# First loads of q and k by pairs of tiles, turned by 64x64 products, and second heads' v shifted by one chunk

## The chip, the cores and the metric

The kernel runs on one core of one Trainium2 chip. The metric is device time in microseconds (us) of one execution. Three executions of the kernel before took 480.24, 480.55 and 480.69 us, a median of 480.55. One more execution was taken with the hardware profiler.

A core has a matrix engine (PE, or TensorE), three engines for elementwise work (DVE or VectorE, ACT or ScalarE, POOL or GpSimd), and an engine that here only issues transfers (SP). Each has its own instruction stream. In this kernel every engine works through its stream in the order in which the program was written; an instruction that has to wait holds up all that stands behind it on its engine.

## The reference

Two stages, one behind the other, all in fp32:

```python
# q, k, v: 8 batches, 8 heads, 576 tokens, 64 numbers a head; chunks of 64 tokens
scores = matmul(q_c, k_c.transpose(0, 1, 2, 4, 3)) / 8       # inside each chunk
attn   = exp(scores - max(scores)); attn /= sum(attn) + 1e-9
x      = matmul(attn, v_c)              # rearranged to 4608 tokens x 512
h      = x @ w_in                       # 512 -> 1024
e      = exp(h - max(h))
solu   = h * e / (sum(e) + 1e-9)
ln     = (solu - mean(solu)) / sqrt(var(solu) + 1e-6) * g_ln
out    = ln @ w_out                     # 1024 -> 512
```

w_in and w_out come as 64-bit floats, so they are 4 MB each.

## The kernel before, in words

The 4608 tokens are 36 **tiles** of 128 tokens: two chunks of 64 tokens, all 8 heads. A tile passes through these steps, named by the word that stands for each in the list `START`, which orders the first tiles by hand; behind the word comes the tile.

- `n`: q and k of a tile are loaded in natural layout, one token a partition, all heads beside one another. In DRAM a head's tokens lie one behind the other, so that each packet of the load is one token of one head: 64 numbers, 256 bytes.
- `N`: four 128x128 transposes on PE (`po<-ident,nat`, two heads in each) for q or for k, and one copy out of PSUM to `qT` or `kT`, on ACT, or on DVE for the pairs in `NV_DVE`.
- `S`: scores, 16 products of 64x64 (`sx<-kT,qT`). `A`: maximum, subtraction (both DVE) and exponential (ACT). `B`: sum and reciprocal (DVE), then the product with it (POOL).
- `T`: the weights are transposed on PE (`po<-ident,e`) and copied to `attn_t`. `V`: 16 products with v (`sy<-attn_t,v_sb`), and the copy of the result: to `x_f` for tiles 0 and 1, else split in a high and a low part, `x_h` and `x_l`.
- `v`: the load of v. `T` leaves the weights of half of the heads, here the second heads of the pairs, with the tile's two chunks swapped over the partitions. For tiles 0 to 5 v is therefore loaded in three transfers: the first heads over 128 partitions, and the second heads in two of 64 partitions each, swapped (four in tile 4, where the batch ends in the middle).
- `M`: h of a tile, into both banks of `ph`, of which there is one. Tiles 0 and 1 use 8 fp32 products `ph<-w_a,x_f`; from tile 2 on three reduced-precision products stand for one, 24 in all (`wi_l,x_h`, `wi_h,x_h`, `wi_h,x_l`). M of tile 0 comes in four pieces, one for each quarter of the weights, so that it can start before all of them are there.
- `X`, `Y`: maximum of h (DVE `h_nmax`), exponential (ACT `z`), product with h (DVE `z`), and the scaling. The next tile's `M` needs `ph`, so it waits for the product on DVE.
- `z`, `Z`: the transposing of z; `F`: the products with w_out (`po<-wo_h,z_h` and so on).
- `P`, `P0`, `P1`: loads of the weights (`w_raw`, 1 MB each; 0 comes in two halves). `c`, `C`, `t`, `D` turn 64-bit floats to fp32 and split them: `c` is a clamp on `w_raw` (DVE or POOL, by `CL_DVE`) and a pass on ACT, `C` a shift and a `SCALAR_TENSOR_TENSOR` on DVE, `t` and `D` the high and low parts. `g` and `G` load and turn g_ln.
- `W`: two 128x128 products of the identity whose result nobody reads, into one held `ph` tile.

A word that stands several times in `START` goes on with its step where it had stopped: `N:0:1` the second time is the copy. Word order sets the order on every engine and of SP's transfers at once. Behind `START` a loop over tiles 5 to 35 does the rest; from there on q and k come in the packets of 128 bytes (`q_st`, `k_st`) and are turned on DVE, and the loop is not touched by the change.

All instructions pass through one helper, so that the profile puts them at line 50; they are told apart by the names of their tiles. `po` is two tiles of one PSUM bank, `ph` one tile of two banks, `sx` and `sy` one tile each.

Of the kernel before, what the change touches and what calls it, by code (L numbers as in the profile page):

```python
# [21 lines left out]
N:2:1 T:0 N:2:1 A:1 C:1 C:0 B:1 V:0 B:1 P:3 N:3:0 t:2 S:2 N:3:1 V:0 M:0 A:2 N:3:0 c:3 N:3:1 T:1  # L22
T:1 S:3 D:2:1 P:4 n:4 c:3 v:1 M:0 A:3 G C:3 A:2 n:5 M:0 G C:3 c:4 M:0 P:5 A:3 B:2 N:4:1 N:4:0
t:3 c:4 n:6 B:2 N:4:1 v:2 N:4:0 V:1 v:3 B:3 B:3 X:0 T:2 T:2 P:6 X:0 Y:0 C:4 N:5:0 C:4 S:4 N:5:0
D:2:0 A:4 V:1 c:5 P:7 T:3 T:3 D:3:0 N:5:1 M:1 t:1 D:1:0 N:5:1 V:2 t:4 A:4 c:5 t:0 D:4:0 N:6:1
D:4:1 D:0:0 N:6:0 C:5 B:4 Y:0 V:2 n:7 X:1 B:4 D:1:1 N:6:1 V:2 X:1 S:5 N:6:0 T:4 D:0:1 V:3 T:4
Y:1 v:4 z:0:0 n:8 D:3:1 z:0:1 A:5 z:0:1 C:5 z:0:0 c:6 z:0:0 M:2 A:5 N:7:0 R:0 B:5 v:7 V:3 B:5
t:5 v:5 Q:2 q:8 z:0:1 c:6 T:5 S:6 V:3 D:5:0 V:4 X:2 C:6 N:7:0 N:7:1 T:5 q:8 c:7 X:2 F N:7:1 C:6
V:4 Y:2 N:8:0 c:7 t:6 D:5:1 C:7 M:3 V:4 C:7 N:8:0 D:6:0 Y:2 N:8:1 t:7 q:8 D:7:0 Y:1 D:6:1 A:6
N:8:1 V:5 D:7:1 X:3 n:9 S:7 Z:2 R:2 z:1:0 F A:7 X:3 Y:3 A:7 z:1:0 F B:7 Y:3 A:6 V:5 o:0 M:4 B:7  # L30
z:1:1 v:6 B:6 Z:3 o:0 z:1:1 z:1:0 z:1:1 B:6 R:3 X:4 F V:5 N:9:0 N:9:0 X:4 F N:9:1 U:6 U:7 R:1 F
Y:4 o:1 N:9:1 Y:4 o:1 R:4 q:8
"""


# [23 lines left out]
def chunk_attention_then_solu_ffn(  # L59
# [178 lines left out]
    AT = const.tile([P, 2, 2, H, 32], F32, name="attn_t")  # L240
# [61 lines left out]
    def load_v(i):  # L302
        V[i] = work.tile([P, H, D], F32, name="v_sb", bufs=4)
        if i < TURNS:

            parts = [(0, p0, p1, b, s) for p0, p1, b, s in tile_parts(i)]
            for c in range(2):
                b, n = chunk_of(i, c)
                parts.append((1, (1 - c) * CH, (2 - c) * CH, b, n * CH))
            for j, p0, p1, b, s in parts:  # L310
                sync.dma_start(
                    V[i][p0:p1, j * HP:(j + 1) * HP, :],
                    v[b, j::2, s:s + p1 - p0, :].rearrange("h t d -> t h d"),
                )
# [593 lines left out]
```

## Time and profile before

| | |
|---|---|
| runs | 480.24, 480.55, 480.69 us |
| profiled execution | 481.02 us |
| its span, first to last instruction | 479.2 us |
| PE busy | 464.7 us, 97% of the span |
| DVE, ACT, POOL busy | 363.9 us (76%), 251.7 us (53%), 157.4 us (33%) |
| chain that ended last | PE 91%, DMA 4%, SP's queue 3% |
| transfers | 195076 packets, 72.57 MB, mean 151 GB/s |

The profiled execution takes 1.8 us more than its span, for what lies before the first and behind the last instruction. A row of the timeline gives the start, the time from there to the end of the group, the engine, and the operation as out<-in; what the engine stood idle before it and what ended that is in brackets. An fp32 product of PE appears as two records (the 16 products of S are x32, the 8 of M of tile 1 are x16), a transpose and a reduced-precision product as one. Beside PE's busy share, PEclk gives the clock that was granted to it, as a part of full speed. The first 60 us are the ones to look at: there PE stands still or waits for a part of the time, and from there on the chain of waits is PE with hardly a break.

### The profile page before, as it was taken

The numbers are of one execution on the slowest core, as the hardware profiler recorded it, in microseconds if no ns is written. First come the engines' busy times: TensorE is split into PE (matmuls) and PEld (weight loads), VectorE is DVE, ScalarE is ACT, GpSimd is POOL, SyncE is SP. The second block draws the span as 40 slices with busy tenths as digits, with TensorE's granted clock in tenths as the row PEclk, the third lists the DMA queues.
The fourth block names the chain that finished last, engine by engine and source line by source line (L and its number), as shares of the span: only waits on it lengthen the run. The fifth ranks groups of instructions, "written<-read, shape, count | busy, mean of one in ns | idle before, by whom it ended". The sixth has DMA issues, their size and how long they took to land.

```text
span 479.2 us, 11042 instructions
## 1 busy us (share of the span) xinstructions
PE 464.7 (97%) x4189; PEld 380.1 (79%) x4189; DVE 363.9 (76%) x508; ACT 251.7 (53%) x406; POOL 157.4 (33%) x304
## 2 busy tenths in 40 slices
PE   5699999999999999999999999999999999999997
PEld 5556788888888888888888888888888888888876
DVE  1879986697878787878787878797979797945430
ACT  2668784546454645454545555454545455554451
POOL 1255557350505050505050505032515141413300
PEclk9799999999999999999999999999999999999999
DMA  9998999787886878596348595958644434334211
GB/s 265 261 231 216 255 137 195 169 194 156 176 174 168 155 179 145 147 174 165 83 131 163 135 186 124 190 134 180 149 111 111 112 104 118 98 101 112 66 45 44
DMA packets 195076, 72.57 MB, mean 151 GB/s; under 512 B 179208, under 2 KB 179728, under 8 KB 194640
## 3 DMA queue, kind: packets, MB, share of 16 engines
q1 hardware_dynamic: 188608, 59.15, 55.8%
q0 software_dynamic: 6272, 12.60, 10.2%
q8 instruction: 33, 0.54, 0.5%
q14 instruction: 19, 0.16, 0.1%
q10 hardware_dynamic: 144, 0.13, 0.1%
HBM read 37.23 MB, written 9.44 MB: 97 GB/s over the span
## 4 chain that ended last, share of the span: by engine, by line
PE 91%; DMA 4%; SPq 3%; issue 1%; DVE 0%; ACT 0%; DVEq 0%; ACTq 0%
PE po L50 43%; PE ph L50 39%; PE sx L50 5%; PE sy L50 3%; SPq L50 3%; DMA nat<-in_q_dram 3%; DMA nat<-in_k_dram 1%; DMA v_sb<-in_v_dram 1%; ACT z L50 0%; DVE h_nmax L50 0%; ACT z_h L50 0%; DVE o_sb L50 0%; DVE z L50 0%; DVEq L50 0%; ACTq L50 0%
## 5 line engine op out<-in xcount | busy, mean ns | idle before, releaser
L50 PE MATMUL po<-wo_l,z_h 128*128 128x512 f32 x280 | 111.1, 397 | 0.1
L50 PE MATMUL po<-wo_h,z_l 128*128 128x512 f32 x280 | 109.6, 391 | 0.0
L50 PE MATMUL po<-wo_h,z_h 128*128 128x512 f32 x280 | 109.3, 390 | 0.0
L50 ACT ACTIVATE z<-ph,h_nmax 128x1024 f32<-128x1024 f32 x36 | 40.2, 1118 | 130.3 <-DVE h_nmax L50 130.0
L50 PE MATMUL ph<-wi_l,x_h 128*128 128x512 f32 x272 | 106.0, 390 | 0.0
L50 PE MATMUL ph<-wi_h,x_h 128*128 128x512 f32 x272 | 105.8, 389 | 0.0
L50 POOL TENSOR_TENSOR u<-ssq,eps 128x1 f32<-128x1 f32 x36 | 6.8, 190 | 215.8 <-ACT sq L50 215.7
L50 POOL DMA_DIRECT2D z_t<-z_b x136 | 67.9, 507 | 17.5 <-DVE z_b L50 12.4
L50 PE MATMUL ph<-wi_h,x_l 128*128 128x512 f32 x272 | 72.7, 389 | 0.0
L50 DVE TENSOR_REDUCE h_nmax<-ph 128x1 f32<-128x1024 f32 x36 | 44.0, 1223 | 35.5 <-PE ph L50 35.5
L50 PEld LDWEIGHTS po<-wo_l,z_h 128*128 128x128 f32 x280 | 52.5, 188 | 11.8 <-ACT z_h L50 0.5
L50 PEld LDWEIGHTS po<-wo_h,z_l 128*128 128x128 f32 x280 | 52.6, 188 | 11.5 <-DVE z_l L50 0.4
L50 PEld LDWEIGHTS po<-wo_h,z_h 128*128 128x128 f32 x280 | 52.6, 188 | 10.4
L50 PEld LDWEIGHTS ph<-wi_h,x_l 128*128 128x128 f32 x272 | 51.1, 188 | 10.6
L50 PEld LDWEIGHTS ph<-wi_l,x_h 128*128 128x128 f32 x272 | 51.1, 188 | 10.6
L50 PEld LDWEIGHTS ph<-wi_h,x_h 128*128 128x128 f32 x272 | 51.1, 188 | 10.5
L50 DVE TENSOR_TENSOR z_l<-z_t,z_h 128x1024 fp32r<-128x1024 f32 (+1 forms) x35 | 40.8, 1164 | 21.3 <-ACT z_h L50 21.3
L50 DVE SCALAR_TENSOR_TENSOR z<-ph,z 128x1024 f32<-128x1024 f32 x36 | 43.9, 1220 | 12.8 <-ACT z L50 12.7
L50 ACT ACTIVATE z<-z,z_sum 128x1024 f32<-128x1024 f32 x34 | 39.2, 1153 | 22.1 <-DVE z L50 21.6
L50 DVE STREAM_TRANSPOSE z_b<-z 128x1024 f32<-128x1024 f32 x33 | 39.9, 1208 | 6.4 <-DMA attn_t<-a_b 3.4
L50 ACT ACTIVATE o_sb<-po,r 128x512 f32<-128x512 f32 (+1 forms) x36 | 24.3, 675 | 32.1 <-POOL r L50 24.9
L50 ACT ACTIVATE sq<-z 128x1024 bf16<-128x1024 f32 x36 | 37.6, 1043 | 0.4 <-POOL z L50 0.4
(85 smaller groups left out, 625.4 us busy)
## 6 DMA issues: line engine op xcount, KB each, us to landing
out_dram<-o_sb SPq DMA_DIRECT2D x35, 256.0 KB, 2.5
z_t<-z_b POOLq DMA_DIRECT2D x128, 64.0 KB, 2.9
z_t<-z_b SPq DMA_DIRECT2D x128, 64.0 KB, 2.9
v_sb<-in_v_dram SPq DMA_DIRECT2D x27, 256.0 KB, 4.0
q_st<-in_q_dram SPq DMA_DIRECT2D x96, 72.0 KB, 3.1
k_st<-in_k_dram SPq DMA_DIRECT2D x96, 72.0 KB, 2.9
w_raw<-in_moe_w_out_dram SPq DMA_DIRECT2D x4, 1024.0 KB, 7.9
attn_t<-a_b POOLq DMA_DIRECT2D x60, 64.0 KB, 3.7
```

The lines of the kernel that those rows point to most:

```text
L50: ins = make(*args, **kwargs)
```

## The change

q and k of the first six tiles are no longer loaded tile by tile. `m:p:x` loads q (x = 0) or k (x = 1) of tiles 2p and 2p + 1 in one transfer of 512 KB: a partition takes two neighbouring tokens, which lie side by side in DRAM for each head, so that a packet has 512 bytes. Pair 2 is in two parts, since the batch ends inside it. Pairs 0 and 2 go to `nat`, pair 1 to two work tiles (`nat_z`) which the exponentials use later. `E:p:x` turns such a pair by 32 products of 64x64 with the identity (ordinary products where the transposes were), which leave even and odd tokens apart in PSUM: in two `po` banks, or in `ph` for k of pairs 0 and 1. `H:i:x` copies a tile out of it and puts the tokens back in order by writing every second number. Of the twelve copies five are on DVE (before: one of twelve).

The second heads' v for tiles 0 to 5 is loaded shifted by one chunk: one transfer over 128 partitions holds the second chunk of this tile and the first chunk of the next, and `V` takes what it needs from two neighbouring tiles. The first chunk of tile 0 has its own small tile `v_first`, in the place of the padding. That is two transfers a tile where there were three.

Tiles 6 to 9 keep `n` and `N`. The list `START` is in another order throughout, `warm` takes its `ph` tile anew each time, and a few steps sit on other engines: clamps of weights 3, 4 and 5 on POOL, the copies to `x_f` on DVE, the turned weights of tile 2 copied on ACT, one scaling of z on ACT instead of POOL and one the other way, and one low part on POOL.

```diff
 START = """
-W:1 n:0 N:0:1 W:2 N:0:0 n:1 N:0:0 W:5 N:0:1 P:2 P0 N:1:0 P1 S:0 N:1:1 W:4 A:0 c:2 P:1 N:1:0 A:0
-n:2 N:1:1 S:1 B:0 c:2 c:0 g N:2:0 c:0 C:2 c:1 c:1 C:2 C:0 C:1 A:1 W:19 v:0 n:3 B:0 T:0 N:2:0
...
+m:0:0 m:0:1 P0 E:0:0 P:1 H:0:0 P1 H:1:0 E:0:1 H:0:1 S:0 H:1:1 c:1 m:1:0 c:1 A:0 C:1 A:0 c:0 B:0
+m:1:1 S:1 W:3 E:1:0 c:0 B:0 H:3:0 A:1 W:11 P:2 g c:2 A:1 H:2:0 v:0 P:3 C:0 P:4 C:0 E:1:1 C:1
...
-    NV_DVE = ((1, 1), (6, 1), (9, 1),)
-    MEAN_POOL = (3, 4,)
-    CL_DVE = (1, 3, 4, 5,)
-    TV_DVE = (2,)
+    NV_DVE = ((0, 0), (0, 1), (2, 1), (3, 1), (4, 1), (7, 1), (9, 1),)
+    MEAN_POOL = (1, 3,)
+    CL_DVE = (1,)
+    TV_DVE = ()
...
-    XV_DVE = ()
+    XV_DVE = (0, 1,)
...
-    const.tile([P, 336], F32, name="pad")
+    v_first = const.tile([P, H // 2, D], F32, name="v_first")
...
+    PAIRS = 3
+    IN_H = ((0, 1), (1, 1))
...
+    def load_pairs(m, x):
+        t = pair_of(m, x).rearrange("p h s d -> p h (s d)")
+        at = [chunk_of(2 * m, c) for c in range(4)]
+        c0 = 0
+        for c in range(1, 5):
+            if c == 4 or at[c][0] != at[c0][0]:
+                b, n = at[c0]
+                sync.dma_start(
+                    t[c0 * 32:c * 32],
+                    (q, k)[x][b, :, n * CH:(n + c - c0) * CH, :].rearrange(
+                        "h (p s) d -> p h (s d)", s=2
+                    ),
+                )
+                c0 = c
...
+    def turn_pairs(m, x):
...
+        for hp in range(HP):
+            for s in range(2):
+                for j in range(2):
+                    for r in range(2):
+                        rows = slice(r * CH, (r + 1) * CH)
+                        pe.matmul(
+                            banks[r][j * D:(j + 1) * D, hp, s],
+                            t[rows, 2 * hp + j, s],
+                            ident[rows, rows],
+                            start=True,
+                            stop=True,
+                        )
...
+    def take_pairs(i, x):
+        to = (QT, KT)[x][i].rearrange("p a (t s) -> p a s t", s=2)
+        if (i, x) in NV_DVE:
+            dve.tensor_copy(out=to, in_=QK[i, x])
+        else:
+            act.copy(to, QK[i, x])
...
-            parts = [(0, p0, p1, b, s) for p0, p1, b, s in tile_parts(i)]
-            for c in range(2):
-                b, n = chunk_of(i, c)
-                parts.append((1, (1 - c) * CH, (2 - c) * CH, b, n * CH))
+            parts = [(V[i][p0:p1, :HP], 0, b, s) for p0, p1, b, s in tile_parts(i)]
+            if i == 0:
+                parts.insert(0, (v_first[CH:], 1, 0, 0))
+            (b0, n0), (b1, _) = chunk_of(i, 1), chunk_of(i, 2)
+            last = i == TURNS - 1
+            assert last or b0 == b1
+            parts.append((V[i][:CH if last else P, HP:], 1, b0, n0 * CH))
...
-                    h, row = 2 * hp + j, c
+                    h, row, of, at = 2 * hp + j, c, V[i], 2 * hp + j
                     if i < TURNS:
-                        h, row = 2 * hp + c, j ^ c
+                        h, row, at = 2 * hp + c, j ^ c, j * HP + hp
+                        if j > c:
+                            of, at = (V[i - 1], at) if i else (v_first, hp)
...
-        if not idle:
-            idle.append(ps_h.tile([P, 2, HALF], F32, name="ph"))
+        idle = ps_h.tile([P, 2, HALF], F32, name="ph")
```

Three places show what the new list moves. First the queue of SP, from the first transfer on. Before:

```order
L50 DMA nat<-in_q_dram 128x8x64
L50 DMA nat<-in_k_dram 128x8x64
L50 DMA nat<-in_q_dram 128x8x64
L50 DMA nat<-in_k_dram 128x8x64
L50 DMA w_raw<-in_moe_w_in_dram 128x2048
L50 DMA w_raw<-in_moe_w_in_dram 128x1024 x2
L50 DMA w_raw<-in_moe_w_in_dram 128x2048
L50 DMA nat<-in_q_dram 128x8x64
L50 DMA nat<-in_k_dram 128x8x64
```

and with the change:

```order
L50 DMA nat<-in_q_dram 128x8x128
L50 DMA nat<-in_k_dram 128x8x128
L50 DMA w_raw<-in_moe_w_in_dram 128x1024
L50 DMA w_raw<-in_moe_w_in_dram 128x2048
L50 DMA w_raw<-in_moe_w_in_dram 128x1024
L50 DMA nat_z<-in_q_dram 128x8x128
L50 DMA nat_z<-in_k_dram 128x8x128
L50 DMA w_raw<-in_moe_w_in_dram 128x2048
```

The same first megabyte of q and k comes in two transfers instead of four; the 1 MB weight load second in the new row of weights (`P:1`) is the one whose clamp stands on DVE.

Then DVE from its first instruction. Before, the first scores' maximum comes first and the clamp on `w_raw` seventh:

```order
L50 TENSOR_REDUCE s_nmax<-sx 128x8
L50 TENSOR_TENSOR e_99<-sx,s_nmax 128x4x128
L50 COPY kT<-po 128x512
L50 TENSOR_REDUCE s_sum<-e_99 128x8
L50 RECIPROCAL s_rinv<-s_sum 128x8
L50 TENSOR_SCALAR w_a<-w_a 128x1024
L50 TENSOR_SCALAR w_a<-w_raw 128x1024
```

With the change two copies come first, then the clamp, then the maximum:

```order
L50 COPY qT<-po 128x4x2x64
L50 COPY kT<-ph 128x4x2x64
L50 TENSOR_SCALAR w_a<-w_raw 128x1024
L50 TENSOR_REDUCE s_nmax<-sx 128x8
L50 TENSOR_TENSOR e_99<-sx,s_nmax 128x4x128
L50 TENSOR_SCALAR w_a<-w_a 128x1024
L50 TENSOR_REDUCE s_sum<-e_99 128x8
L50 RECIPROCAL s_rinv<-s_sum 128x8
L50 TENSOR_REDUCE s_nmax<-sx 128x8
L50 TENSOR_TENSOR e_100<-sx,s_nmax 128x4x128
L50 TENSOR_SCALAR w_a<-w_a 128x1024
L50 SCALAR_TENSOR_TENSOR w_a<-w_raw,w_a 128x1024 x2
```

and behind them, up to the copy that the first products with the weights need:

```order
L50 COPY kT<-ph 128x4x2x64 x2
L50 TENSOR_REDUCE s_sum<-e_100 128x8
L50 RECIPROCAL s_rinv<-s_sum 128x8
L50 TENSOR_REDUCE s_nmax<-sx 128x8
L50 TENSOR_TENSOR e_99<-sx,s_nmax 128x4x128
L50 TENSOR_SCALAR w_a<-w_a 128x1024
L50 COPY x_f<-sy 128x512
```

So the clamp has moved from behind the first tile's softmax to ahead of it, and the copy to `x_f`, which was on ACT, now stands on DVE behind all of these.

Last PE from the first to the last piece of M of tile 0 and on towards M of tile 1. Before:

```order
L50 MATMUL ph<-w_a,x_f 128x512 x2
L50 MATMUL po<-ident,e_100 128x128 x4
L50 MATMUL sx<-kT,qT 64x64 x16
L50 MATMUL ph<-w_a,x_f 128x512 x2
L50 MATMUL po<-ident,g_row 128x8
L50 MATMUL ph<-w_a,x_f 128x512 x4
L50 MATMUL po<-ident,nat 128x128 x8
L50 MATMUL sy<-attn_t,v_sb 64x64 x16
L50 MATMUL po<-ident,e_99 128x128 x4
L50 MATMUL po<-ident,nat 128x128 x4
L50 MATMUL sx<-kT,qT 64x64 x16
```

With the change:

```order
L50 MATMUL ph<-w_a,x_f 128x512 x2
L50 MATMUL po<-ident,e_100 128x128 x4
L50 MATMUL ph<-w_a,x_f 128x512 x4
L50 MATMUL po<-ident,nat 64x64 x32
L50 MATMUL ph<-w_a,x_f 128x512 x2
L50 MATMUL po<-ident,e_99 128x128 x4
L50 MATMUL sy<-attn_t,v_sb 64x64 x16
L50 MATMUL po<-ident,nat 64x64 x32
L50 MATMUL sy<-attn_t,v_sb 64x64 x16
L50 MATMUL sx<-kT,qT 64x64 x16
L50 MATMUL po<-ident,e_100 128x128 x4
```

One turn of scores and the turn of g_ln have left this stretch for an earlier place, one more turn of values is in it, and two turns by 32 products stand where four by 4 transposes stood. Some 90 rows from its first on, each engine's order is the same as before.

More of the change, by code (lines that the diff above doesn't have):

```diff
@@ L19 @@
 START = """
-W:1 n:0 N:0:1 W:2 N:0:0 n:1 N:0:0 W:5 N:0:1 P:2 P0 N:1:0 P1 S:0 N:1:1 W:4 A:0 c:2 P:1 N:1:0 A:0
-n:2 N:1:1 S:1 B:0 c:2 c:0 g N:2:0 c:0 C:2 c:1 c:1 C:2 C:0 C:1 A:1 W:19 v:0 n:3 B:0 T:0 N:2:0
[L22 to L32, printed above, removed]
+m:0:0 m:0:1 P0 E:0:0 P:1 H:0:0 P1 H:1:0 E:0:1 H:0:1 S:0 H:1:1 c:1 m:1:0 c:1 A:0 C:1 A:0 c:0 B:0
+m:1:1 S:1 W:3 E:1:0 c:0 B:0 H:3:0 A:1 W:11 P:2 g c:2 A:1 H:2:0 v:0 P:3 C:0 P:4 C:0 E:1:1 C:1
+H:3:1 t:0 v:1 m:2:0 D:0:1 T:0 H:2:1 B:1 G B:1 T:0 c:3 S:2 W:2 c:2 t:1 V:0 W:1 W:5 A:2 C:2 V:0
+v:2 C:2 t:2 S:3 M:0 c:3 A:2 T:1 M:0 A:3 G C:3 m:2:1 P:5 c:4 T:1 M:0 B:2 C:3 A:3 D:2:1 E:2:0 B:3
+c:4 H:4:0 B:2 H:5:0 P:6 C:4 B:3 t:3 M:0 D:2:0 T:2 V:1 X:0 D:1:1 T:2 E:2:1 V:1 D:3:0 H:4:1 X:0
+V:2 Y:0 V:2 c:5 S:4 C:4 Y:0 T:3 v:3 A:4 n:6 n:7 c:5 C:5 C:5 P:7 M:1 T:3 A:4 Q:2 D:1:0 H:5:1
+N:6:0 S:5 t:4 t:5 B:4 v:4 V:2 N:6:1 X:1 c:6 N:6:0 D:5:0 B:4 A:5 n:8 T:4 N:6:1 N:7:0 T:4 X:1
+D:0:0 N:7:1 N:7:1 D:4:0 N:7:0 V:3 c:7 V:3 Y:1 D:3:1 S:6 z:0:0 z:0:0 z:0:1 V:3 z:0:1 A:5 A:6 c:7
+z:0:1 B:5 M:2 c:6 D:4:1 q:8 q:8 n:9 R:0 C:7 D:5:1 z:0:0 N:8:0 N:8:0 X:2 V:4 S:7 N:8:1 B:5 X:2
+C:7 N:8:1 V:4 Y:1 F T:5 v:5 Y:2 q:8 C:6 Y:2 t:7 D:7:0 C:6 M:3 t:6 A:7 D:6:0 Z:2 T:5 D:6:1 R:2
+N:9:0 F V:4 X:3 q:8 N:9:0 A:6 X:3 Y:3 D:7:1 A:7 V:5 R:1 B:6 z:1:0 V:5 F z:1:0 Y:3 v:6 o:0 z:1:0
+M:4 B:6 z:1:1 B:7 B:7 Z:3 z:1:1 V:5 X:4 o:0 z:1:1 F X:4 F U:6 N:9:1 Y:4 Y:4 F U:7 o:1 R:3 v:7
+R:4 N:9:1 o:1
 """
@@ L284, in chunk_attention_then_solu_ffn, with pair_of @@
     nat = work.tile([P, 2, 2, H, D], F32, name="nat", tag="z_t")
+    PAIRS = 3
+    IN_H = ((0, 1), (1, 1))
+    middle = {}
+    def pair_of(m, x):
+        if m == 1:
+            if x not in middle:
+                middle[x] = work.tile([P, FF], F32, name="nat_z", tag="z")
+            t = middle[x]
+        else:
+            t = nat[:, x].rearrange("p x h d -> p (x h d)")
+        return t.rearrange("p (h s d) -> p h s d", h=H, s=2)
+    def load_pairs(m, x):
[13 more added lines that the diff above has]
+    def turn_pairs(m, x):
+        for i in (2 * m, 2 * m + 1):
+            if i not in QT:
+                qk_tiles(i)
+        t = pair_of(m, x)
+        if (m, x) in IN_H:
+            both = ps_h.tile([P, 2, HALF], F32, name="ph")
+            banks = [both[:, r] for r in range(2)]
+        else:
+            banks = [bank() for _ in range(2)]
+        banks = [y.rearrange("p (a s t) -> p a s t", s=2, t=CH) for y in banks]
+        for hp in range(HP):
[10 more added lines that the diff above has]
+                        )
+        for r in range(2):
+            QK[2 * m + r, x] = banks[r]
+    def take_pairs(i, x):
+        to = (QT, KT)[x][i].rearrange("p a (t s) -> p a s t", s=2)
+        if (i, x) in NV_DVE:
+            dve.tensor_copy(out=to, in_=QK[i, x])
+        else:
+            act.copy(to, QK[i, x])
     def tile_parts(i):
@@ L304, in load_v @@
         if i < TURNS:
[L306 to L310 removed]
+            parts = [(V[i][p0:p1, :HP], 0, b, s) for p0, p1, b, s in tile_parts(i)]
[5 more added lines that the diff above has]
+            parts.append((V[i][:CH if last else P, HP:], 1, b0, n0 * CH))
+            for to, j, b, s in parts:
                 sync.dma_start(
[L312 to L313 removed]
+                    to, v[b, j::2, s:s + to.shape[0], :].rearrange("h t d -> t h d")
                 )
@@ L454, in values @@
                         s[j * D:(j + 1) * D, c, hp],
-                        V[i][rows, j * HP + hp if i < TURNS else h, :],
+                        of[rows, at, :],
                         AT[rows, :, i % 2, h, :],
@@ L523, in ffn_in @@
             )
-    idle = []
     def warm(x):
-        if not idle:
-            idle.append(ps_h.tile([P, 2, HALF], F32, name="ph"))
+        idle = ps_h.tile([P, 2, HALF], F32, name="ph")
         for n in range(2):
             pe.matmul(
-                idle[0][:, n, x % 4 * P:(x % 4 + 1) * P], ident, ident, start=True, stop=True
+                idle[:, n, x % 4 * P:(x % 4 + 1) * P], ident, ident, start=True, stop=True
             )
@@ L778, in chunk_attention_then_solu_ffn @@
         "v": load_v, "g": load_g, "G": turn_g, "Q": load_batch, "q": load_some,
-        "N": turn_natural, "S": scores, "A": start_softmax, "B": softmax_b,
+        "N": turn_natural, "m": load_pairs, "E": turn_pairs, "H": take_pairs, "S": scores, "A": start_softmax, "B": softmax_b,
         "T": attn_transpose, "U": attn_turn, "V": start_values, "c": unit_scale,
```

4 lines of the change are left out of this document (2 added, 2 removed).

## The prediction

> **What bounds the kernel now.** I read the page first, then the chain of waits, then stretches of ten microseconds, and at last single engines over the first 60 us. The page gives the span, and the shares of the chain that ended last:
>
> ```profile
> span 479.2 us, 11042 instructions
> PE 91%; DMA 4%; SPq 3%; issue 1%; DVE 0%; ACT 0%; DVEq 0%; ACTq 0%
> ```
>
> The chain is PE wherever it can be. What is not PE lies early, as the chain's own rows show:
>
> ```profile
> 8.15 9.06 DMA nat<-in_q_dram
> ...
> 31.88 3.48 DMA nat<-in_q_dram
> ...
> 54.67 2.86 DMA v_sb<-in_v_dram
> ...
> 58.25 2.75 PE po L50 x15
> ```
>
> From 58.25 us on nothing but PE follows until the tail, and the change leaves the order there alone. So it can win or lose only ahead of that point: what counts is by how much PE gets earlier through the same work. The stretches (columns: stretch, its length, busy PE, PEld, DVE, ACT, POOL, then PEclk, DMA share, GB/s) say how much waiting there is to win:
>
> ```profile
> 15.70:22.50 6.80, 5.16 (x51) 4.74 (x52) 6.33 (x8) 3.99 (x7) 0.26 (x1) 0.50 0.83 180
> 30.00:40.00 10.00, 9.54 (x101) 5.86 (x100) 8.65 (x14) 7.83 (x13) 5.47 (x5) 1.00 0.90 222
> 50.00:60.00 10.00, 9.06 (x103) 7.37 (x102) 9.49 (x13) 7.98 (x16) 5.05 (x5) 1.00 0.97 226
> ```
>
> PE lacks 0.46 us in the second and 0.94 us in the third; in the first it had half its clock. DVE is busy for 8.65 and 9.49 of ten, so it is the next engine. PE's own timeline puts names to this:
>
> ```profile
> 17.34 1.09 PE L50 MATMUL po<-ident,nat 128*128 128x128 f32 x4 [4.24 <-DMA nat<-in_q_dram]
> 18.22 1.06 PE L50 MATMUL ph<-ident 128*128 128x128 f32 x4
> ...
> 23.94 1.88 PE L50 MATMUL ph<-w_a,x_f 128*128 128x512 f32 x4
> ...
> 32.51 1.04 PE L50 MATMUL po<-ident,nat 128*128 128x128 f32 x8
> 33.47 0.98 PE L50 MATMUL sy<-attn_t,v_sb 64*64 64x64 f32 x32
> 34.38 0.66 PE L50 MATMUL po<-ident,e 128*128 128x128 f32 x4
> 35.50 0.63 PE L50 MATMUL po<-ident,nat 128*128 128x128 f32 x4 [0.46 <-DMA nat<-in_q_dram]
> 36.06 0.69 PE L50 MATMUL sx<-kT,qT 64*64 64x64 f32 x32
> 36.69 0.65 PE L50 MATMUL po<-ident,e 128*128 128x128 f32 x4
> ...
> 37.61 7.03 PE L50 MATMUL ph<-w_a,x_f 128*128 128x512 f32 x16
> 44.58 0.69 PE L50 MATMUL sy<-attn_t,v_sb 64*64 64x64 f32 x32
> 55.08 0.63 PE L50 MATMUL po<-ident,nat 128*128 128x128 f32 x4 [0.45 <-DMA nat<-in_q_dram]
> 57.58 0.68 PE L50 MATMUL sy<-attn_t,v_sb 64*64 64x64 f32 x26 [0.49 <-DMA v_sb<-in_v_dram]
> ```
>
> PE stands 4.24 us for tile 2's q, reaches M of tile 0 at 23.94, and waits again for transfers at 35.50, 55.08 and 57.58. All four are q, k or v in small packets. But the first wait is not simply lost time: M of tile 0 also needs DVE's work.
>
> **The start, up to M of tile 0.** Today's wait for tile 2's q goes, because q and k of tiles 0 and 1 take the queue for less time and only weights stand ahead of the next pair. What is late next is DVE. In the change its order is clamp (`w_a<-w_raw`), maximum, subtraction, shift, sum, reciprocal, maximum, subtraction, shift, two SCALAR_TENSOR_TENSOR, two copies of k, sum, reciprocal, maximum, subtraction, shift, then the copy to `x_f` that M of tile 0 reads. The clamp needs weight load 1, and everything waits behind it. DVE's rows price the links, start to start (the copy by its own time):
>
> ```profile
> 11.58 0.68 DVE L50 COPY kT<-po 128x512 f32<-128x512 f32 x1
> ...
> 17.89 1.29 DVE L50 TENSOR_SCALAR w_a<-w_a 128x1024 uint32<-128x1024 uint32 x2
> 19.09 0.70 DVE L50 TENSOR_REDUCE s_nmax<-sx 128x8 f32<-128x512 f32 x1
> 19.89 0.69 DVE L50 TENSOR_TENSOR e<-sx,s_nmax 128x512 f32<-128x512 f32 x1
> 20.50 2.54 DVE L50 SCALAR_TENSOR_TENSOR w_a<-w_raw,w_a 128x1024 uint16<-128x1024 uint32 x2
> 22.93 0.68 DVE L50 TENSOR_REDUCE s_sum<-e 128x8 f32<-128x520 f32 x1
> 23.64 0.20 DVE L50 RECIPROCAL s_rinv<-s_sum 128x8 f32<-128x8 f32 x1
> 23.76 0.64 DVE L50 TENSOR_REDUCE s_nmax<-sx 128x8 f32<-128x512 f32 x1
> ```
>
> Clamp and shift 0.60 each (1.20 for the pair at 17.89), maximum 0.80, subtraction 0.61, two SCALAR_TENSOR_TENSOR 2.43, sum 0.71, reciprocal 0.12, copy 0.68. Four of 0.60, three maxima 2.40, three subtractions 1.83, 2.43, two sums and reciprocals 1.66, three copies 2.04: 12.8 us from weight load 1 to `x_f`. No row shows a copy that writes every second number; I take the plain copy's 0.68, and for the upper end that such a copy takes as long as one of the maxima, 0.80, which adds 0.4 over the three.
>
> When is weight load 1 there? Today it ends the first 4 MB; with the change it ends the first 2.5 MB (q and k of pair 0, half of load 0, load 1). Two rows: POOL's first clamp, and the rates of the first 10 us in 40 slices:
>
> ```profile
> 10.96 1.10 POOL L50 TENSOR_SCALAR w_a<-w_raw 128x1024 f32<-128x1024 f32 x1 [9.53 <-DMA w_raw<-in_moe_w_in_dram]
> GB/s 0 0 0 0 0 0 0 69 161 96 261 288 287 288 282 229 184 194 227 243 227 232 221 217 219 382 305 140 262 459 328 426 360 393 492 393 311 361 459 377
> ```
>
> Today 1 MB of 256-byte packets and 1 MB of weights had landed by 10.96. While q and k run alone the rate is some 225 GB/s, with 8 KB packets some 390. The half megabyte more costs 1.3 us at 390, so 12.3 us if 512-byte packets are no faster than 256-byte ones. If they run at the weights' rate, 1.05 MB takes 2.7 us instead of 4.7: 10.3. No row shows the rate of this load; I take 10.8, nearer the fast end, since a packet twice as long lies between the two kinds and the number of packets halves.
>
> [...]
>
> So `x_f` is there at 10.8 + 12.8 = 23.6, and M of tile 0 starts at 23.7 instead of 23.94: **0.2 us won**, out of 4.24 us of waiting removed. PE's first part (two turns, scores) ends near 10 us as today and lies beside this.
>
> **Behind that start.** PE's work that is left changes a little. The scores of tile 3 (0.63, from 36.06 to 36.69) and the turn of g_ln (0.12, a fourth of a turn of four) are done before. Tiles 4 and 5 are turned by two times 32 products instead of four times 4 transposes. The nearest row for 64x64 products is the scores': 16 cost 0.63, so 32 cost 1.26, two turns 2.52; four turns today are twice 0.96 (32.51 to 33.47), 1.92. Sum: 0.75 − 0.60 = 0.15, **0.2 won**. The lower end of a turn is 0.96, as today, the upper the half-clock price, 1.26 × 0.88/0.48 = 2.3 (0.88 is the step from 17.34 to 18.22).
>
> M of tile 0 takes 8.57 us from 23.94 to 32.51 today. The same products for tile 1 take 6.97 (37.61 to 44.58); with a turn of e (four transposes, 0.48), scores (0.63) and g_ln (0.12) inside that is 8.20. The rest, **0.4**, is its wait for the last quarter of the weights. With the change DVE comes to that quarter, by its order, behind `x_f`, a SCALAR_TENSOR_TENSOR, a maximum, a subtraction, a shift, a sum and a reciprocal, and ends the second SCALAR_TENSOR_TENSOR some 5.3 us behind `x_f`, at 28.9; PE, with six products, the turn of e and one of 32 products ahead (5.2 + 0.48 + 1.26), comes to it at 30.6. The wait goes.
>
> The three waits for transfers, 0.46 and 0.94 us, go if the queue's front gains more than they are long. Twelve loads of 256 KB take 1.16 us each at 225 GB/s; at 328, which the 10.8 us above imply (1.05 MB in 3.2 us instead of 4.7), they take 0.8, together 4.3 us less. v keeps its bytes and packet size but needs fewer issues. The pairs' q and k stand ahead of tile 5's v and of tile 6's q, so both are some 4 us earlier, against 0.45 and 0.49: **1.4 won**. At the slow end nothing is won in the queue and these waits stay.
>
> New waits: M of tile 1 needs `ph` back from the product on DVE,
>
> ```profile
> 35.68 1.21 DVE L50 SCALAR_TENSOR_TENSOR z<-ph,z 128x1024 f32<-128x1024 f32 x1
> ```
>
> which ends at 36.9 today, 4.4 us behind M of tile 0. With the change M ends at 32.4 (23.7 + 6.97 + 0.48 + 1.26), `ph` is back at 36.8, and PE's work ahead of M of tile 1 (two turns of e 1.0, two of values 1.3, scores 0.63, one pair turn 1.26) is done at 36.6. They meet within **0.2**, which I count as lost, for this place and the like one ahead of M of tile 3; up to 1.0 if DVE, which gets pair copies here, comes later to the product.
>
> Sum: 0.2 + 0.2 + 0.4 + 1.4 − 0.2 = 2.0 us. The profiled execution took 481.02 (span 479.2 and 1.8 around it), so 479.0 there; the median of the runs is 0.47 below it, so **478.5 us**. Own range: clamp at 12.3 or 10.3, +1.5 or −0.5; new waits up to 0.8 more; turns −0.6; not all at once, 477.5 to 480.5.
>
> **Rivals.**
>
> *The saving stays hidden.* Weight load 1 lands at 12.3, so M of tile 0 starts at 25.2, 1.5 later than forecast, and 0.5 remains: 480.0. Copies at 0.80 take 0.4 more: 480.4, no change. For it speaks that at 50 to 60 us the DMA share is 0.97 while only 226 GB/s move, with v's packets as before; against it that the first 10 us show two rates by packet size.
>
> *The clock stays low, slower.* Place: M of tile 0. Today PE idled 4.24 us up to 17.34, and over 15.7 to 22.5 had half its clock; that came back after 5.2 us of unbroken work, just ahead of M. With the change PE has only some 8 us of pieces in the 13 us before M (four pair turns, four of scores, e, values), each behind DVE or a transfer, so the work that brought the clock back today is broken up. If it is half until the second piece of M has ended (six products and e: 5.2 + 0.48 = 5.7 us at full clock, 10.4 at 0.88/0.48), 4.7 are lost and 2.0 won: 480.55 + 2.7 = 483.3. It decides from 2.4 us of PE's work at half clock on, where the 2.0 are eaten up. Against it: of five steps `W` in the new list three stand close ahead of M.
>
> *The clock is low for a short while.* The same, but only for the first two products and e (1.74 + 0.48 = 2.2 us of work): 1.8 lost, 480.4, no change.
>
> [...]
>
> *Larger gain.* Weight load 1 lands at 10.3 and PE's turns cost 0.96 where I have 1.26: M starts at 23.2, and 0.6 more goes with two turns; DVE's clamps for loads 3, 4 and 5, now on POOL (0.60 each), let it be in time ahead of M of tiles 1 and 3, so that 0.2 is not lost. 2.0 + 0.5 + 0.6 + 0.2 = 3.3: 477.2.
>
> **How the numbers follow.** Forecast 0.44, hidden 0.18, short clock 0.07, long clock 0.16, larger gain 0.13, others 0.02. About 0.2%, 1.0 us, is what can be told from no change here. Faster are the forecast and the larger gain; hidden and the short clock are within; slower is the long clock with the others. Faster 0.57, same 0.25, slower 0.18. The range reaches from 476.7 to 481.3, and leaves out most of the long clock and a little below.
>
> **What would show it.** PE's first `ph<-w_a,x_f` near 23.7, with DVE the releaser and no row of 4 us idle for q. DVE's clamp on `w_raw` at 10.3 to 11.3. PEclk 1.00 over 24 to 33; 0.5 to 0.8 there means the slower case. M of tile 1 at 36.8 instead of 37.61, with a turn of values more behind it. No waits for `nat` or `v_sb` at 50 to 60. The prediction is wrong if M of tile 0 starts past 25, if a turn of 32 products takes over 1.5 us at full clock, or if PE's idle from 24 to 60 stays at 1.4 us.

## The result: 0.7% slower

The changed kernel took 483.87 us (median of four, 482.88 to 484.50) against 480.39 for the kernel before: a ratio of 1.0074, 95% interval 1.0051 to 1.0096. Repeated beside more runs it was 1.0067 (1.0046 to 1.0088). The prediction had said 478.5, faster.

The profiled execution took 482.88 us. Its page:

```profile
span 480.8 us, 11698 instructions
q8 instruction: 36, 0.59, 0.6%
PE 91%; DVE 4%; DMA 2%; issue 1%; SPq 0%; ACT 0%; DVEq 0%; ACTq 0%
```

In the chain DMA went from 4% to 2% and SP's queue from 3% to 0, as meant; DVE, which had no share, has 4%. There are 656 instructions more than before, and 36 transfers of instructions where there were 33: 0.59 MB in 36 packets is 16 KB each. The stretches from 10 to 60 us:

```profile
10.00:20.00 10.00, 7.49 (x191) 6.56 (x184) 8.01 (x12) 5.53 (x8) 2.27 (x3) 0.66 1.13 335
20.00:30.00 10.00, 9.26 (x128) 5.92 (x127) 9.02 (x14) 6.31 (x9) 6.93 (x6) 1.00 1.07 281
30.00:40.00 10.00, 8.15 (x240) 5.67 (x238) 6.95 (x12) 5.23 (x9) 9.08 (x7) 1.00 1.02 300
50.00:60.00 10.00, 9.91 (x170) 8.19 (x169) 9.76 (x17) 7.29 (x14) 7.33 (x8) 1.00 0.78 125
```

The 0.94 us that PE lacked at 50 to 60 us are gone (9.91 busy). But it now lacks 1.85 us at 30 to 40, where it lacked 0.46. PE's timeline names the place:

```profile
18.14 1.63 PE L50 MATMUL ph<-ident,nat_z 64*64 64x64 f32 x64
...
25.12 1.98 PE L50 MATMUL ph<-w_a,x_f 128*128 128x512 f32 x4
...
30.91 1.16 PE L50 MATMUL po<-ident,nat 64*64 64x64 f32 x64
32.00 1.98 PE L50 MATMUL ph<-w_a,x_f 128*128 128x512 f32 x4
...
34.97 0.98 PE L50 MATMUL po<-ident,nat 64*64 64x64 f32 x41
37.48 0.52 PE L50 MATMUL po<-ident,nat 64*64 64x64 f32 x20 [1.52 <-issue]
...
38.84 0.69 PE L50 MATMUL sx<-kT,qT 64*64 64x64 f32 x32 [0.32 <-DVE kT L50]
...
39.98 7.13 PE L50 MATMUL ph<-w_a,x_f 128*128 128x512 f32 x16
```

M of tile 0 starts at 25.12 instead of 23.94, and M of tile 1 at 39.98 instead of 37.61. In between the turn of k of tiles 4 and 5 stops for 1.52 us after 41 of its 64 records, which is in the middle of a product (two records each), and the view names no releaser ("issue"). The 13 waits of PE with a named releaser in the profiles of before and of the changed kernel (0.24 to 5.06 us), for transfers and other engines, all stand ahead of the first record of a product; this one does not. Behind the turn stand a copy of k on DVE, and behind that DVE's product which gives `ph` back to M of tile 1.

The first transfers did what was forecast, as DVE's timeline shows:

```profile
10.49 0.69 DVE L50 TENSOR_SCALAR w_a<-w_raw 128x1024 f32<-128x1024 f32 x1 [0.96 <-DMA w_raw<-in_moe_w_in_dram]
...
19.85 1.29 DVE L50 COPY kT<-ph 128x512 f32<-128x512 f32 x2 [1.12 <-PE ph L50]
...
23.96 0.68 DVE L50 COPY x_f<-sy 128x512 f32<-128x512 f32 x1
...
28.32 1.48 DVE L50 TENSOR_SCALAR w_a<-w_a 128x1024 uint32<-128x1024 uint32 x1
...
38.09 0.69 DVE L50 COPY kT<-po 128x512 f32<-128x512 f32 x1 [2.25 <-PE po L50]
38.70 1.22 DVE L50 SCALAR_TENSOR_TENSOR z<-ph,z 128x1024 f32<-128x1024 f32 x1
```

The clamp starts at 10.49 (forecast 10.8), but `x_f` ends at 24.64 instead of the forecast 23.6.

### The profile page after: what moved, and what is told of

Same layout as the page of the kernel before. It is cut to its first block, busy times and chain, and to the rows that moved or that the text cites. A ratio compares the mean times of both kernels' runs of the same rounds, so it can differ in the third digit from the quotient of the medians.

```text
span 480.8 us, 11698 instructions
## 1 busy us (share of the span) xinstructions
PE 465.7 (97%) x4525; PEld 380.9 (79%) x4525; DVE 367.3 (76%) x509; ACT 249.0 (52%) x401; POOL 164.3 (34%) x309
## 4 chain that ended last, share of the span: by engine, by line
PE 91%; DVE 4%; DMA 2%; issue 1%; SPq 0%; ACT 0%; DVEq 0%; ACTq 0%
PE ph L50 42%; PE po L50 41%; PE sx L50 5%; PE sy L50 3%; DMA w_raw<-in_moe_w_in_dram 2%; DVE w_a L50 1%; DVE z L50 1%; DVE kT L50 1%; DVE h_nmax L50 1%; DVE wo_l L50 1%; SPq L50 0%; DVE e L50 0%; DVE s_nmax L50 0%; ACT z L50 0%; DVE z_l L50 0%
## 5 line engine op out<-in xcount | busy, mean ns | idle before, releaser
L50 POOL DMA_DIRECT2D z_t<-z_b x136 | 67.7, 505 | 16.9 <-DVE z_b L50 12.9
L50 PEld LDWEIGHTS po<-wo_h,z_h 128*128 128x128 f32 x280 | 52.6, 188 | 10.3
L50 POOL DMA_DIRECT2D attn_t<-a_b x60 | 29.4, 496 | 25.1 <-PE ph L50 18.2
```

The costliest lines, as they stand in the source:

```text
L50: ins = make(*args, **kwargs)
```

## The experiments

In the table each row is one profiled execution: the start of M of tiles 0, 1 and 3 from PE's timeline, and the span. From M of tile 3 to the end of the span it is 417.5 to 418.5 us in all of them but e7_pair0_only (419.1), so that what is lost is lost ahead of it. Times are medians, except in the last group; the median of the kernel before, run beside them, stands at the head of a group (e5 to e8 were run beside other runs of it than a2 to e4, with the same median). In some of these kernels the helper stands at line 49.

| kernel | M0 | M1 | M3 | span | time |
|---|---|---|---|---|---|
| before | 23.94 | 37.61 | 60.87 | 479.2 | |
| changed | 25.12 | 39.98 | 63.01 | 480.8 | |
| *beside before at 480.85* | | | | | |
| a2_same_again | 24.62 | 40.58 | 63.85 | 481.5 | 484.11 |
| e2_no_warms | 24.53 | 40.17 | 63.16 | 480.9 | 484.04 |
| e3_256_bytes | 27.97 | 41.46 | 64.19 | 481.9 | 484.57 |
| e4_shift | 26.91 | 43.38 | 66.27 | 483.9 | 485.87 |
| e5_two_natural | 25.06 | 39.75 | 62.79 | 480.3 | 482.15 |
| e6_v_alone | 24.92 | 38.59 | 60.34 | 478.5 | 479.97 |
| e7_pair0_only | 23.48 | 37.80 | 60.08 | 479.2 | 480.75 |
| e8_pairs01_v | 26.27 | 39.11 | 60.88 | 479.4 | 480.95 |
| *beside before at 480.37* | | | | | |
| f1_q_first | 25.15 | 38.01 | 60.64 | 478.6 | 480.18 |
| f3_pair0_v | 23.95 | 37.10 | 58.90 | 477.3 | 478.82 |
| f4_k_on_act | 25.18 | 39.17 | 61.87 | 479.4 | 481.69 |
| *one execution each* | | | | | |
| f2_weights_later | 28.91 | 42.91 | 66.08 | 483.8 | 485.92 |
| a3_look | 24.55 | 41.34 | 64.39 | 482.0 | 484.05 |
| a4_look | 24.53 | 41.45 | 65.34 | 483.2 | 485.18 |

My theory was code loading: PE's instructions come in blocks of 16 KB, a turn by 32 products uses 128 instructions (64 weight loads, 64 products) in 1.1 us, and the next block is late. The rivals were a buffer or late transfer at this turn, the clock, and DVE.

**The changed kernel again.** No edit.

> The changed kernel, unaltered, to see what varies between its executions: the four so far took 482.88 to 484.50 us, and the profiled one was the fastest. Theory of code loading (PE stands 1.5 us in the middle of tile 4 and 5's turn of k because its next 16 KB of instructions have not come): the stall stands again at the 41st of the 64 records of that turn, give or take two, but lasts another time, 1 to 4 us, and the time goes with it. Theory of the clock: the stall is the same, and what varies is the granted clock over 10 to 30 us. Either way the median is 483 to 485.

The stall stands at the same record, and the clock is halved behind it. PE's timeline, and two stretches (the first ends where the stall does):

```profile
37.25 0.52 PE L50 MATMUL po<-ident,nat 64*64 64x64 f32 x20 [1.78 <-issue]
```

```profile
36.00:38.00 2.00, 0.75 (x49) 0.75 (x51) 0.14 (x1) 0.00 (x0) 2.00 (x3) 0.98 1.09 345
38.00:41.30 3.30, 3.17 (x56) 2.49 (x48) 3.30 (x5) 2.16 (x3) 1.58 (x2) 0.50 0.98 199
```

**Without W.**

```diff
-m:1:1 S:1 W:3 E:1:0 c:0 B:0 H:3:0 A:1 W:11 P:2 g c:2 ...
+m:1:1 S:1 E:1:0 c:0 B:0 H:3:0 A:1 P:2 g c:2 ...
```

(and the other three taken out too)

> The changed kernel without its five steps W (ten products of the identity, 40 PE instructions less). By the clock theory W costs more than it brings: between 13.8 and 24.6 us they take four times 1.15 us at half clock ahead of turns for which DVE waits, so without them M of tile 0 starts 0.5 to 1.5 us before 25.12. If they keep the clock up, it falls instead and M of tile 0 starts later, with PEclk under 1.0 over 20 to 30. By the theory of code loading the stall moves 40 instructions on, to the 61st record of the same turn or just behind it. If the stall is a wait for a buffer, it stays at the 41st.

Its PE timeline:

```profile
24.53 1.98 PE L50 MATMUL ph<-w_a,x_f 128*128 128x512 f32 x4 [1.21 <-DVE x_f L50]
...
37.98 0.33 PE L50 MATMUL po<-ident,nat 64*64 64x64 f32 x3 [1.59 <-issue]
```

The stall has moved from the 41st to the 61st record: 20 records and 20 weight loads, just the 40 instructions that were taken out. A buffer or a transfer would not move with the count. M of tile 0 starts where it does in three of the four profiles of the changed kernel (24.53 to 24.62), PEclk was 1.00 over 20 to 30, and the time is the same: W neither cost nor brought anything that can be told, against the first theory of the expectation.

**256-byte packets.**

```diff
-                sync.dma_start(
-                    t[c0 * 32:c * 32],
...
+                for s in range(2):
+                    sync.dma_start(
+                        t.rearrange("p h (s d) -> p h s d", s=2)[c0 * 32:c * 32, :, s],
...
```

> The changed kernel with each pair load split in two transfers, even tokens and odd tokens, so that packets have 256 bytes again; all else the same. If 512-byte packets are what moves the queue's front, DVE's clamp on weight load 1 goes from 10.49 to 11.9 to 12.5 and M of tile 0 is 1 to 2 us later. If the early queue is bound by something else than packet size, the clamp stays within 0.3 of 10.49.

```profile
13.12 0.69 DVE L50 TENSOR_SCALAR w_a<-w_raw 128x1024 f32<-128x1024 f32 x1 [3.05 <-DMA w_raw<-in_moe_w_in_dram]
```

The clamp is 2.6 us later (expected: 1.4 to 2.0): packet size is what moves the front, by more than the 2.0 us between my bounds of 12.3 and 10.3. (The edit also doubles the number of these transfers, which was not tried apart.) M of tile 0 is 2.85 us later, yet the time only 0.46: here the turn of tiles 4 and 5 runs later against the queue and has no stall, and M of tile 1 follows M of tile 0 by 13.5 us instead of 14.9.

**Shifted blocks.**

```diff
-m:0:0 m:0:1 P0 E:0:0 ...
+K:24 m:0:0 m:0:1 P0 E:0:0 ...
+        for _ in range(n):
+            pe.matmul(few[:CH, 0, :CH], ident[:CH, :CH], ident[:CH, :CH], start=True, stop=True)
```

> The changed kernel with 24 small products of the identity (64x64, 96 PE instructions) ahead of everything, in the 5 us in which PE waits for its first data anyway. By the theory of code loading the end of a block of 256 instructions moves from the middle of tile 4 and 5's turn of k to a place ahead of it, and the fetch that was late is asked for during the products with the weights, 2 to 3 us earlier against the work: the stall of 1.5 us shrinks below 0.5, M of tile 1 starts at 38.2 to 38.8 instead of 39.98, and the median falls by 1 to 2 us. If the stall belongs to that turn itself (a buffer, a late transfer), it stays at the 41st record and the time stays.

The time rose instead: the small products took 5.3 us, to 6.7, and four stalls stand where there was one. From its PE timeline:

```profile
19.87 0.68 PE L50 MATMUL ph<-ident,nat_z 64*64 64x64 f32 x26 [0.98 <-issue]
...
26.53 0.45 PE L50 MATMUL sx<-kT,qT 64*64 64x64 f32 x13 [0.75 <-issue]
...
38.35 0.34 PE L50 MATMUL sy<-attn_t,v_sb 64*64 64x64 f32 x6 [1.53 <-issue]
...
42.61 0.34 PE L50 MATMUL sx<-kT,qT 64*64 64x64 f32 x7 [1.57 <-issue]
```

Counted in PE's stream from its first instruction in the trace, weight loads, products and its own waits for semaphores together, they stand behind 705, 961, 1217 and 1473 instructions: exactly 256 apart. The stall of the changed kernel stands behind 1217 in all four profiles of it, that of e2_no_warms too. So the stalls stood at steps of 256 instructions, whichever turn, scores or values stood there: one packet of 16 KB a step.

The trace has the packets too. Taken in order, the first is for the mark at 449, the next for that at 705, and so on. In the 16 profiles PE passes 545 such marks, none sooner than 2.3 us behind the start of its packet. All eleven stalls of this kind, 0.46 to 2.44 us long, stand at such marks, passed 2.3 to 2.9 us behind it; the other marks were passed 2.7 us behind it or later, most of them much later. So PE stood where its next block had only just been fetched. That the expected gain did not come fits: the marks stay and the work moves past them by 96 instructions, so that other blocks are late. The expectation "the stall shrinks" was wrong, the one that it leaves that turn was right.

**Tiles 4 and 5 in the old way.**

```diff
-... v:1 m:2:0 ... m:2:1 ... E:2:0 ... H:4:0 ... H:5:0 ... E:2:1 ...
+... v:1 n:4 ... n:5 ... N:4:0 N:5:0 ... N:4:0 ... N:5:0 ... N:4:1 N:5:1 ...
```

> The changed kernel with tiles 4 and 5 loaded and turned as before (256-byte packets, four transposes a turn), at the same places of the list: some 220 PE instructions less between 30 and 39 us. By the theory of code loading the stall in that turn is gone, M of tile 1 starts 13.2 to 13.8 us behind M of tile 0 instead of 14.9 to 16, and the time falls by 1 to 2 us, to 482 to 483. If PE waited for the late data of pair 2 rather than for its instructions, the natural loads, which are no faster, make it wait as long, and the time stays at 484.

The stall is gone and the time fell by 2 us to 482.15, but a wait stands in its place: `nat<-in_q_dram`, 2.22 us up to 33.58, since k of tile 4 was loaded ahead of q of tile 5. So M of tile 1 came 14.7 us behind M of tile 0, not the 13.2 to 13.8 that I had expected. With q of both first (same edit, with a load in the order q, q, k, k):

> As the kernel in which tiles 4 and 5 are loaded and turned in the old way, but with q of both tiles ahead of k of both, as the new list needs them. The wait of 2.2 us for tile 5's q falls below 0.7 by the theory that this wait stood for the stall in the other kernel; M of tile 1 starts at 38.0 to 38.8 and the time is 480.8 to 481.8. If what costs time lies ahead of M of tile 0 or behind M of tile 1, M of tile 1 may come earlier and the time stays at 482.

```profile
32.20 1.98 PE L49 MATMUL ph<-w_a,x_f 128*128 128x512 f32 x4 [0.33 <-DVE w_a L49]
38.01 7.13 PE L49 MATMUL ph<-w_a,x_f 128*128 128x512 f32 x16
```

M of tile 0 starts at 25.15, as in the changed kernel, M of tile 1 at 38.01, 12.9 us behind it, and the ratio to before is 0.9995 (0.9976 to 1.0014). The changed kernel's was 1.0067: pair 2, its loads and turns together, costs 0.7%, all that was lost. The time of 480.18 is below the 480.8 that I had expected at least, but what is left of the change brings nothing that can be told.

**v alone, pair 0 alone, both pairs 0 and 1.** The list of before, with single parts of the change. For v alone: `load_v`, `values` and `v_first` of the change in the kernel before. For pair 0 alone, without v (`warm` stays as in the change here and in the kernels below that have pair 0):

```diff
-W:1 n:0 N:0:1 W:2 N:0:0 n:1 N:0:0 W:5 N:0:1 P:2 P0 N:1:0 P1 S:0 N:1:1 W:4 ...
+W:1 m:0:0 m:0:1 W:2 E:0:0 H:0:0 W:5 H:1:0 E:0:1 H:0:1 P:2 P0 P1 S:0 H:1:1 W:4 ...
```

and for two pairs, with v, also `m:1`, `E:1`, `H:2`, `H:3` for `n:2`, `n:3` and their `N`.

> The kernel before with nothing but the new load of v (second heads shifted by one chunk, two transfers a tile instead of three) and the products that take from two tiles. By the prediction's step on the transfers the wait of 0.49 us for tile 5's v goes and the rest stays: 480.3 to 480.9, no change that can be told. If v's part is what costs the changed kernel its time, this one is at 482 or more.

> The kernel before, its list and its engines, with tiles 0 and 1 alone loaded as a pair in 512-byte packets and turned by 64x64 products (256 records in 1 turn of q and 1 of k), copies on ACT; tiles 2 to 9 and v as before. The queue wins some 1.2 to 1.4 us at its front, which no long DVE chain hides here, since the clamp stands where it stood: M of tile 0 starts at 22.6 to 23.2 instead of 23.94, with no stall of PE without a releaser, and the time is 479.4 to 480.2. By the clock theory PE at half clock takes 2.0 us for each turn, M stays at 23.9 or later and the time at 480.8 or above.

> The kernel before, its list and its engines, with tiles 0 to 3 as two pairs in 512-byte packets, all their copies on ACT, and the new load of v; tiles 4 to 9 as before. If packet size is worth what the first 13 us of the changed kernel show, and its loss comes from the late stall, the clamp ahead of the scores and POOL's clamps, M of tile 0 starts at 22.3 to 23.2 and the time is 478.8 to 480.2. If 64x64 turns cost by the instructions that they need, a stall without a releaser of 0.5 us or more shows between 17 and 30 us and the time is 481 to 483.

Ratios 0.9981 (0.9959 to 1.0003), 1.0008 (0.9983 to 1.0034), 1.0000 (0.9975 to 1.0024): none can be told from no change. v's part is not what costs time, and its wait at 57.58 is gone. With pair 0 M of tile 0 comes 0.46 earlier (expected 0.7 to 1.3). That is less than single profiles differ: in e6_v_alone, whose list is that of before, tile 2's q came at 18.59 instead of 17.34 and M of tile 0 0.98 later. With pairs 0 and 1 M of tile 0 comes later, without a stall:

```profile
17.53 1.99 PE L49 MATMUL po<-ident,nat_z 64*64 64x64 f32 x64 [4.15 <-DMA nat_z<-in_q_dram]
...
26.27 1.98 PE L49 MATMUL ph<-w_a,x_f 128*128 128x512 f32 x4 [1.75 <-ACT x_f L49]
```

The first wait is no longer than that of before (4.24 us, up to 17.34). But the turn took 1.99 us, as at half clock (PEclk 0.78 over 10 to 20 and 0.88 over 20 to 30; a turn at PEclk 1.00 took 1.16 in the changed kernel), where four transposes took 1.09, and the copy to `x_f` on ACT, which stands behind the copies of pair 1's k, ends a second wait of 1.75 us that the kernel before does not have. My expectations of 22.3 to 23.2 for M of tile 0, of 478.8 to 480.2 for this kernel and of 479.4 to 480.2 for pair 0 were wrong, and the stall of the other case did not come.

**Pair 0 with v.** Both edits.

> The kernel before with tiles 0 and 1 alone as a pair, and the new load of v: the two parts whose runs took 480.75 and 479.97 against 480.85 for the kernel before. If their gains add up, 479.4 to 480.2, and the wait of 0.27 us for v is gone; if the gain of either is within what varies, 480.0 to 480.9.

478.82 against 480.37, ratio 0.9964 (0.9943 to 0.9985): faster than both kernels, and below the 479.4 to 480.2 that I had expected. PE's timeline has no stall. M of tile 0 starts where it did before (23.95), M of tile 1 0.5 us earlier:

```profile
37.10 7.10 PE L50 MATMUL ph<-w_a,x_f 128*128 128x512 f32 x16
```

From M of tile 1 to M of tile 3 it takes 21.80 us; the other two kernels with v's new load and the old list take 21.75 and 21.77, pair 0 alone 22.28, the kernel before 23.26. So v's load seems to win about 1.5 us there, which e6_v_alone lost again ahead of M of tile 0; these are single profiles, and why the two parts together win more than the product of their ratios (0.9989) is not shown.

**Weights later.** Two loads of w_out moved in SP's queue, behind v of tile 3 and tile 6.

```diff
-... m:2:1 P:5 c:4 ... H:5:0 P:6 C:4 ... V:2 c:5 ... v:3 A:4 n:6 n:7 ...
+... m:2:1 c:4 ... H:5:0 C:4 ... V:2 v:3 n:6 P:5 P:6 c:5 ... A:4 n:7 ...
```

> The changed kernel with the two loads of 1 MB of w_out that stand behind pair 2's k moved behind v of tile 3 and q and k of tile 6, which SP can issue only when pair 2 has been turned. By the theory that the fetch of instructions waits behind full queues, the 16 KB packet that started at 35.07 starts at 31.3 to 33.5, and the stall at the 41st record is gone or under 0.3 us; the time itself may rise, as the weights come later. If the fetch is late for another reason, it starts at 35 again and PE stands 1.5 us.

The stall at the 41st record is gone; the packet of instructions started at 34.15, later than expected, but 5.2 us behind the start of M of tile 0, where it was 9.95 behind in the changed kernel. But another boundary, in the scores of tile 2, was late here:

```profile
23.14 0.46 PE L49 MATMUL sx<-kT,qT 64*64 64x64 f32 x16 [1.37 <-issue]
...
28.91 2.88 PE L49 MATMUL ph<-w_a,x_f 128*128 128x512 f32 x4
```

It stands behind 705 instructions, one of the same marks. M of tile 0 was 3.8 us later (its first four records took 2.88 us instead of 1.98, and PEclk was 0.70 over 20 to 30), so that PE's work stood otherwise against the queue: that a full queue delays the fetch was my guess, and is not shown by this.

**Without W, and k's copies on ACT.** f1_q_first with `(2, 1), (3, 1)` out of `NV_DVE` and no `W`.

> The changed list with tiles 4 and 5 in the old way (q first), without the five steps W, and with the copies of k of tiles 2 and 3 on ACT instead of DVE. By the theory that DVE's chain from the clamp on sets M of tile 0, the chain loses 1.3 us of copies: M of tile 0 starts at 23.0 to 23.6, M of tile 1 at 36.6 to 37.6, and the time is 479.0 to 480.2, better than before if at all. If PE's clock decides, it is low over 20 to 30 us without W and M of tile 0 takes longer than 9 us.

It missed: M of tile 0 at 25.18, time 481.69 (ratio 1.0007, 0.9985 to 1.0029). Its stretch and PE row:

```profile
20.00:30.00 10.00, 7.95 (x106) 4.86 (x107) 5.42 (x8) 6.22 (x9) 6.33 (x6) 0.66 0.93 255
```

```profile
21.83 0.58 PE L49 MATMUL sx<-kT,qT 64*64 64x64 f32 x9 [0.46 <-issue]
...
25.18 3.70 PE L49 MATMUL ph<-w_a,x_f 128*128 128x512 f32 x4
```

Here is the clock that I had feared: PEclk was 0.66 over 20 to 30, the first four records of M of tile 0 took 3.70 us instead of 1.98, as at about half clock, and a stall stands behind 705 instructions here too. ACT took the copies late (1.46 us wait for `kT`). That a DVE chain freed of copies brings M forward is not shown.

**Two more profiles of the changed kernel**, for what varies between its executions.

> The changed kernel once more, unaltered, to see where its slower executions lose what the first profile does not show: two profiles so far, spans 480.8 and 481.5 us, against medians of 484 for the time. By the theory of code loading the stall between the 40th and 42nd record of the turn is there again, 1.3 to 3 us long, and what the second profile showed behind it, PE at less than full clock over 30 to 50 us, comes and goes. If executions differ elsewhere, M of tile 1 starts at 40 to 40.6 in all of them and the difference stands behind it.

> The changed kernel a fourth time, for the same question. By the theory of code loading the stall stands within two records of the 41st, and M of tile 1 starts 14.5 to 17 us behind M of tile 0; if the executions differ elsewhere, that distance is 14.9 as in the first profile and the time differs all the same.

The stall of the second of them, a4_look, and a stretch behind it:

```profile
38.37 0.52 PE L50 MATMUL po<-ident,nat 64*64 64x64 f32 x20 [2.19 <-issue]
```

```profile
40.10:43.40 3.30, 3.30 (x31) 2.15 (x22) 3.20 (x6) 2.55 (x3) 0.00 (x0) 0.50 0.95 193
```

In the first of them, a3_look, the clock stayed at 1.00, but PE waited for pair 2's q ahead of its turn, as it did for 0.78 us in a4_look:

```profile
31.29 1.22 PE L50 MATMUL po<-ident,nat 64*64 64x64 f32 x64 [0.91 <-DMA nat<-in_q_dram]
...
38.84 0.52 PE L50 MATMUL po<-ident,nat 64*64 64x64 f32 x20 [2.44 <-issue]
```

In all four profiles of the changed kernel the stall stands behind the 41st record and lasts 1.52, 1.78, 2.44 and 2.19 us; in two (a2_same_again, a4_look) PE has half its clock for 3.4 us behind it. M of tile 1 comes 14.9, 16.0, 16.8 and 16.9 us behind M of tile 0, and the spans are 480.8, 481.5, 482.0 and 483.2. The first profile was the luckiest of the four: its span is 1.6 us above that of before, the others 2.3 to 4.0, and the medians differ by 3.3 to 3.5.

## Why the prediction was wrong

**Where the sum failed.** The forecast was 2.0 us less; the span of the first profile is 1.6 us more. Up to M of tile 0 it is 1.2 us more (forecast: 0.2 less), from there to M of tile 1 1.2 us more (forecast: 0.6 less), behind that 0.8 us less (forecast: 1.2 less). In f1_q_first, without pair 2, the three are 1.2 more, 0.8 less and 1.1 less: there only the first was off.

**What PE waits for today, and the transfers: right in the main.** In the first profile of the changed kernel the waits of 1.4 us for q, k and v went; in two of the other three PE waits 0.91 and 0.78 us for pair 2's q. The clamp came at 10.49 for 10.8. My bounds were too near: 256-byte packets put it at 13.12, not 12.3.

**`x_f` 12.8 us behind the clamp: too short, by 1.35 us.** It took 14.15. The chain priced DVE's own work and took nothing for waits inside it. 1.12 us is a wait for the turn of pair 1's k: PEclk was 0.66 over 10 to 20, the turn took 1.63 instead of 1.1, and two W of 1.22 us stood ahead of it. Where that wait is absent (e2_no_warms) the chain still took 14.0: one shift there, from 22.49 on, took 1.39 instead of 0.69 while POOL worked beside it (`e`, 22.27 to 23.33), and five other links took 0.1 to 0.2 us more than priced. So the 4.24 us of waiting did turn into DVE's chain, but M of tile 0 moved back, by 1.2 us in the first profile and 0.6 to 0.7 in the other three, instead of forward by 0.2. That is 0.8 to 1.4 us against the forecast of 23.7, the second term that was mis-sized.

**A turn of 32 products at 1.26 us: right in time, wrong in kind.** At full clock it took 1.1 (30.91 to 32.00 in the changed kernel, PEclk 1.00 over 24 to 33). Its 128 instructions were the cost that I left out: six turns need 768 where twelve turns of transposes needed 96. This is the step that failed most: the new waits, of which the prediction says "They meet within 0.2, which I count as lost". By that M of tile 1 stands 13.1 us behind M of tile 0; it stood 14.9 to 16.9 behind, and 12.9 in f1_q_first, without pair 2's turns. The term missing from the sum is a stall of 1.5 to 2.4 us where a block of instructions comes late, plus in half of the profiles a halved clock, in half the wait for pair 2's q, and 0.3 us for the copy of k that stands between the turn and the scores. No rival had it. Whether the stall brings on the halved clock was not tried.

**The rivals.** Hidden saving: half true, since f1_q_first, with all but pair 2, is no faster than before. Clock: not at its place (PEclk was 1.00 from 24 to 33 in the changed kernel), but behind the stall in two of four profiles. In f4_k_on_act it came as in the short case: the first two products lost 1.7 us, for the 1.8 forecast. That unbroken work brings the clock back, as the long case had it, no run shows: in the changed kernel PE worked in pieces ahead of M of tile 0, and PEclk was 1.00 over 20 to 30. The stretch behind M of tile 3 kept its length within 0.5 us, as assumed. Two of the three signs of being wrong came: M of tile 0 past 25 (25.12, in the first profile alone), and PE's idle from 24 to 60 us, which rose from 1.4 to 2.2 us.

**What stays open.** What sets the start of the fetch. The packets started at 35.07, 34.73, 36.55 and 36.02 in the four profiles, and PE went on 2.3 to 2.5 us later each time; when PE asks for a block the trace does not show. And M of tile 0 is 0.5 to 0.6 us later in the first profile than in the other three, where the turn of pair 1's k took 1.16 us instead of 1.63. PEclk does not settle this: it gives 1.00 over 10 to 20 for two of the three and for e2_no_warms, yet the first turn of pair 1 took 1.99 us in each of them, as at half clock. Why the clock came back earlier there was not tried.
